# Two transformer layers on one core: a new written-out order for all queues, the alternate homes and the PSUM banks

## The chip, the core and the metric

One NeuronCore of a Trainium2 chip runs the program. It has five engines that each work through a queue of their own in order: PE (TensorE, matmuls), ACT (ScalarE, exponentials and gelu), DVE (VectorE), POOL (GpSimd) and SP (SyncE, which here only issues DMAs). They wait for each other through semaphores. The metric is the device time of one execution in microseconds (us); three runs of the kernel before took 441.66, 441.85 and 443.46 us, median 441.85.

## The reference

One attention block and one MLP block, applied twice with the same weights, each behind a layernorm without scale and with a residual sum. There are 2,048 tokens of width 512, 32 heads of 16, and an MLP of width 1,792. Each token attends to itself and the 255 tokens before it.

```python
def attn(x):                                   # A_x: 1 x 2048 x 512, bfloat16
    q, k, v = heads(x @ wqkv)                  # 32 heads of 16
    s = where(0 <= i - j < 256, q @ k.T / 4, -1e9)
    return merge(softmax(s) @ v) @ wo
def mlp(x):
    return gelu_tanh(x @ w1 + b1) @ w2 + b2    # 512 -> 1792 -> 512

x = A_x
for _ in range(2):
    x = x + attn(layernorm(x))
    x = x + mlp(layernorm(x))
```

## The kernel before, in words

The tokens stand as 16 tiles of 128; two layers make 32 tile steps, numbered tau. Attention goes by blocks of two tiles: 16 blocks b, eight of each layer. The MLP goes by ten jobs J of two or four tiles.

The function writes the program down as 3,098 steps with names (keys), each with what it reads and writes. The keys, with the lines of the profile:

- `bs`, `ba` (L599, L601): statistics of a layernorm on DVE; `vp`, `pw` (L611, L617): its inverse root, the first on POOL or DVE, the second on POOL; `xn` (L627): the normalised tile on DVE.
- `tx` (L632): a DMA that transposes `xn` into xnTA (for attention) or xnTB (for the MLP); for the first and last tiles `tp` (L639) on PE and an evacuation `te` instead.
- `q`, `k`, `v` (L653, in `lnq` and `kv`): projections on PE, followed by `qe`, `ke`, `ve` (L588 or L590, L687), which take them out of PSUM; `vs` (L702): two DMAs that swap the halves of V.
- `scB_G` (L754): scores of block B, visit G. A visit fills four PSUM banks; two exponentials `ex` (L761, ACT) empty them; `mk` (L782, DVE or POOL) multiplies by the mask. A block has ten visits (five at the start of a layer).
- `pv` (L804): the product with V, for half a block; then `od`, `rc`, `nm`, `ot` (L813 to L827): transpose, reciprocal of the row sums, normalisation (DVE or POOL), transpose back; `op` (L653): the output projection; `rs` (L849): the residual sum.
- `mJ_F` (L653): first MLP product of job J for the 128 columns F of 14; `gb` and `ga` (L871, L874): bias on DVE, then gelu on ACT for columns 0 to 5; `ge` (L879): bias and gelu on ACT for the others.
- `y` (L653) and `ya` (L894): second MLP product and residual sum; `xb` (L887, POOL): residual plus bias beforehand; `out` (L898): the store. Of the last tile, tau 31, `y`, `ya` and `out` are cut into two halves of 256 columns, `y31_0` and `y31_256`.
- `ld...`: loads; `ldx` of the input, `ldw` of wqkv, `ldwo`, `ldu0` to `ldu2` the three pieces of W1 (columns F 0 to 5, 6 to 9, 10 to 13), `ldz0` to `ldz3` the four of W2.
- `warm`: 18 matmuls on zeros, of 512 or 32 columns, that read gT and write a PSUM bank nobody uses.

The order of all this isn't found at run time. Three lists are written out: `_ORDER` gives the sequence in which steps are put on their engines' queues, `_ALT` the steps that go to their second home (masks, normalisations and layernorm additions have DVE and POOL, evacuations DVE and ACT), `_BANKS` the PSUM bank of each group in that order. `_Plan.run` reads them:

```python
        for i in _ALT:
            nodes[i]["eng"], nodes[i]["fn"] = nodes[i]["alts"][1]
        banks = iter(_BANKS)
        ...
        for i in _ORDER:
            nd = nodes[i]
            assert nd["deps"] <= seen
            seen.add(i)
            for g, k in nd["alloc"]:
                b = next(banks)
```

`_Sched.op` then gives every step the waits that its reads, writes and bank demand. A step that waits holds up everything behind it on its engine. All 160 DMAs stand in SP's queue.

## Time and profile before

| | |
|---|---|
| median of three runs | 441.85 us |
| span of the profiled execution | 442.4 us |
| PE busy | 416.1 us (94%) |
| ACT busy | 386.4 us (87%) |
| DVE busy | 341.0 us (77%) |
| POOL busy | 212.7 us (48%) |
| DMA | 23.25 MB, 53 GB/s in the mean, 202 GB/s in the first 48 us |

The profiled execution is one of its own, 0.55 us (0.1%) above the median of the three runs. Its page gives busy time by engine, then the chain that ended last, then groups of instructions. In the chain's and groups' lines a tile's name stands for all its buffers; many operations of PE have line 653, since one helper records them all. Idle time of an engine is put down to what ended it. Loads of ACT's function tables are instructions of their own there, 1.28 us each.

### The profile page before, as it was taken

Reading aid. Unit: us, or ns where it says so; the run is one execution under the profiler, and the core shown is the slowest. Engines: PE = TensorE matmul, PEld = TensorE weight load, DVE = VectorE, ACT = ScalarE, POOL = GpSimd, SP = SyncE. Lnnn points to the kernel's source line nnn. Section 1 sums busy time; section 2 is a strip of 40 time slices with the busy share of each in tenths; the row PEclk is TensorE's granted clock in tenths of the full one; section 3 lists DMA queues with packets and bytes.
Section 4 is the critical chain, followed back from the end, with each engine's and each line's share of the span. In section 5 each row is a group of like instructions: output and inputs, shape, how many; then the busy total and the mean of one; then the engine's idle time right before and its main releaser. Section 6 shows DMA issues by size and latency. Waiting matters only on the chain.

```text
span 442.4 us, 16864 instructions
## 1 busy us (share of the span) xinstructions
PE 416.1 (94%) x7523; PEld 233.2 (53%) x7593; DVE 341.0 (77%) x638; ACT 386.4 (87%) x458; POOL 212.7 (48%) x236
## 2 busy tenths in 40 slices
PE   8997999988789997999999999999999999999997
PEld 4555657544444563554455455455555464444675
DVE  7997789788785599967698868877888576746762
ACT  4997999999889999889899989999897988999533
POOL 3566344363442674711575454634728165804411
PEclk9999999999899999999999999999999999999999
DMA  7686422004101012121031021100421014003002
GB/s 234 184 209 185 87 64 45 20 10 69 39 3 25 16 34 56 28 46 24 4 65 31 1 57 26 34 20 10 69 39 20 20 39 105 14 1 81 15 0 73
DMA packets 48116, 23.25 MB, mean 53 GB/s; under 512 B 33196, under 2 KB 48044, under 8 KB 48044
## 3 DMA queue, kind: packets, MB, share of 16 engines
q1 hardware_dynamic: 48044, 22.17, 22.2%
q8 instruction: 60, 0.98, 0.9%
q14 instruction: 12, 0.10, 0.1%
HBM read 8.00 MB, written 2.10 MB: 23 GB/s over the span
## 4 chain that ended last, share of the span: by engine, by line
PE 79%; ACT 11%; DVE 6%; issue 2%; DMA 1%; DVEq 0%
PE ps L653 59%; PE ps L754 9%; PE ps L804 9%; ACT E L761 9%; DVE OD L813 1%; PE ps L539 1%; DVE stat L599 1%; DVE X L849 1%; DMA xnTB<-xn 1%; ACT gT L879 1%; ACT L879 1%; DVE KT L687 1%; DVE E L782 0%; PE ps L639 0%; ACT QT L590 0%
## 5 line engine op out<-in xcount | busy, mean ns | idle before, releaser
L761 ACT ACTIVATE E<-ps 128x1024 bf16<-128x1024 f32 x300 | 284.2, 1033 | 28.7 <-PE ps L754 28.0
L782 POOL TENSOR_TENSOR E<-E,mask 128x512 bf16<-128x512 bf16 (+2 forms) x111 | 120.9, 1106 | 91.3 <-ACT E L761 91.0
L653 PE MATMUL ps<-W_sb,gT 128*128 128x512 bf16 (+1 forms) x434 | 112.2, 373 | 3.2 <-issue 2.2
L653 PE MATMUL ps<-xnTB,W_sb 128*128 128x512 bf16 (+1 forms) x541 | 107.8, 336 | 3.4 <-issue 1.8
L653 PEld LDWEIGHTS ps<-xnTB,W_sb 128*128 128x128 bf16 x560 | 52.0, 98 | 42.9 <-issue 4.1
L653 PE MATMUL ps<-xnTA,Wqkv_sb 128*128 128x256 bf16 x512 | 70.7, 273 | 0.9 <-ACT E L761 0.4
L782 DVE TENSOR_TENSOR E<-E,mask 128x512 bf16<-128x512 bf16 (+2 forms) x125 | 60.1, 500 | 13.3 <-ACT E L761 12.9
L754 PE MATMUL ps<-QT,KT 32*128 32x128 bf16 (+3 forms) x1920 | 60.3, 231 | 9.8 <-ACT E L761 5.6
L653 PEld LDWEIGHTS ps<-W_sb,gT 128*128 128x128 bf16 x462 | 41.2, 98 | 41.1 <-issue 3.6
L754 PEld LDWEIGHTS ps<-QT,KT 32*128 32x128 bf16 x1920 | 28.5, 92 | 59.1 <-ACT E L761 34.9
L653 PEld LDWEIGHTS ps<-xnTA,Wqkv_sb 128*128 128x128 bf16 x512 | 47.4, 98 | 20.2 <-issue 2.9
L813 DVE STREAM_TRANSPOSE OD<-ps 128x1024 f32<-128x1024 f32 x32 | 39.9, 1246 | 21.3 <-PE ps L804 20.7
L887 POOL TENSOR_TENSOR Xb<-X,b2all 128x512 f32<-128x512 bf16 x32 | 37.7, 1180 | 34.3 <-DVE X L894 33.9
L879 ACT ACTIVATE gT<-ps,b1T 128x512 bf16<-128x512 f32 (+1 forms) x80 | 42.6, 609 | 9.5 <-PE ps L653 9.4
L804 PE MATMUL ps<-E,Va 64*17 64x128 bf16 (+3 forms) x1920 | 44.3, 234 | 1.9 <-issue 0.8
L821 POOL TENSOR_TENSOR Nb<-OD,Rc 128x512 bf16<-128x512 f32 x25 | 26.4, 1058 | 38.7 <-DVE Rc L817 29.8
L804 PE MATMUL ps<-E,Vs 64*17 64x128 bf16 (+3 forms) x1920 | 44.9, 234 | 0.0
L599 DVE BATCH_NORM_STATS2 stat<-X 128x6 f32<-128x512 bf16 x64 | 42.9, 679 | 0.5
L804 PEld LDWEIGHTS ps<-E,Va 64*17 64x17 bf16 x1920 | 37.2, 85 | 11.6 <-issue 9.0
L871 DVE TENSOR_SCALAR gT<-ps,b1T 128x512 bf16<-128x512 f32 (+1 forms) x60 | 36.8, 632 | 6.6 <-PE ps L653 6.2
L687 DVE TENSOR_TENSOR KT<-ps,parmask 128x1024 bf16<-128x1024 f32 x32 | 38.7, 1211 | 3.6 <-PE ps L653 3.6
L804 PEld LDWEIGHTS ps<-E,Vs 64*17 64x17 bf16 x1920 | 38.0, 85 | 0.2
(55 smaller groups left out, 348.8 us busy)
## 6 DMA issues: line engine op xcount, KB each, us to landing
Vs<-Va SPq DMA_DIRECT2D x64, 68.0 KB, 2.0
W_sb<-in_B_w_dram SPq DMA_DIRECT2D x4, 512.0 KB, 4.8
out_dram<-X SPq DMA_DIRECT2D x15, 128.0 KB, 1.8
X<-in_A_x_dram SPq DMA_DIRECT2D x3, 512.0 KB
Wqkv_sb<-in_A_wqkv_dram SPq DMA_DIRECT2D x4, 256.0 KB, 4.5
W_sb<-in_B_w_dram SPq DMA_DIRECT2D x2, 384.0 KB, 7.1
W_sb<-in_B_w_dram SPq DMA_DIRECT2D x1, 768.0 KB, 5.0
Wqkv_sb<-in_A_wqkv_dram SPq DMA_DIRECT2D x1, 512.0 KB, 6.7
```

The costliest lines, as they stand in the source:

```text
L599: add("dve", lambda e, B, t=t, k6=k6: e.bn_stats(stat6[:, k6, :], X[:, t, :]), reads=["X%d" % t], writes=["st%d" % k6], key="bs%d" % (k + j))
L653: r = e.matmul(ps[:, B[g][0], cols], lhsT, rhs, start=st, stop=sp)
L687: add("dve", lambda e, B, g=g, i=i: e.tensor_tensor(out=KT[:, kb, 2 * i : 2 * i + 2].rearrange("p c m a q -> p a (c m) q"), in0=ps[:, B[g] ...
L754: x = e.matmul(ps[:, bk[r], o : o + n], KT[rows, kb, c, m].rearrange("p a q -> p (a q)"), QT[rows, c, q : q + n], start=True, stop=True)
L761: add("act", lambda e, B, g_=g_, gi=gi: e.activation(E[:, 2 * gi : 2 * gi + 2, e0 : e0 + 512], ps[:, B[g_][0] : B[g_][0] + 2, :], AF.Exp, ...
L782: fn = lambda e, B: e.tensor_tensor(out=Ew, in0=Ew, in1=Mw, op=ALU.mult)
L804: x = e.matmul(ps[32 * r : 32 * r + VW, B[g][par], c % 2 * 2 * P + lo : c % 2 * 2 * P + hi], V[rows, (2 * b + m // 2) % VR, c * HC + 2 * r ...
L813: add("dve", lambda e, B: e.transpose(OD[:, s].rearrange("p a c q -> p (a c q)"), ps[:, B[g][0] : B[g][0] + 2, :]), reads=["ps:" + g], wri ...
L821: return e.tensor_tensor(out=Nb[:, s, :].rearrange("p (k a d) -> p a k d", a=2, d=Dh), in0=sums[:, :, :, 0:Dh], in1=rc[:, :, :, None].to_b ...
L871: add("dve", lambda e, B, g=g, fc=fc: e.tensor_scalar(out=gT[:, fc, c0 : c0 + M], in0=ps[:, B[g][0], 0:M], scalar1=b1T[:, fc : fc + 1], sc ...
L879: add("act", lambda e, B, g=g, fc=fc: e.activation(gT[:, fc, c0 : c0 + M], ps[:, B[g][0], 0:M], AF.Gelu_apprx_tanh, bias=b1T[:, fc : fc + ...
L887: add("pool", lambda e, B, t=t, xs=xs: e.tensor_tensor(out=Xb[:, xs, :], in0=X[:, t, :], in1=b2all[:], op=ALU.add), reads=["X%d" % t, "b2a ...
```

## The change

All three lists are replaced; the function that writes the steps down, `_Plan` and `_Sched` stay. The diff is numbers alone:

```diff
@@ -165,200 +165,193 @@
 _ORDER = [
-    15, 34, 5, 0, 6, 14, 35, 7, 33, 28, 38, 29, 47, 8, 18, 23, 9, 36, 3, 26, 31, 10, 57, 37, 11, 22, 1, 40, 4, 24,
-    2, 58, 59, 61, 17, 42, 62, 21, 60, 65, 41, 63, 19, 64, 68, 55, 32, 66, 107, 39, 69, 67, 20, 105, 50, 70, 3097,
-    48, 30, 27, 53, 25, 106, 108, 71, 109, 49, 72, 110, 73, 16, 74, 114, 81, 75, 82, 111, 83, 84, 115, 85, 86, 116,
...
+    34, 15, 0, 8, 35, 27, 25, 32, 20, 9, 38, 1, 16, 37, 2, 24, 10, 36, 31, 11, 40, 57, 12, 33, 17, 13, 41, 23, 5, 58,
+    4, 59, 3, 61, 21, 14, 62, 29, 42, 60, 65, 63, 19, 47, 64, 6, 68, 66, 39, 107, 67, 69, 28, 105, 70, 22, 50, 108,
+    30, 81, 106, 82, 109, 7, 83, 110, 84, 71, 72, 3097, 111, 73, 74, 114, 112, 85, 75, 86, 87, 115, 88, 116, 89, 113,
...
 ]
 
 _ALT = [
-    67, 70, 75, 102, 109, 116, 121, 148, 165, 170, 185, 192, 198, 202, 211, 216, 337, 342, 370, 374, 378, 384, 389,
-    393, 398, 402, 406, 407, 412, 421, 437, 554, 571, 576, 585, 590, 595, 608, 609, 613, 634, 654, 687, 691, 696, 710,
...
+    67, 70, 75, 95, 109, 116, 121, 165, 170, 185, 192, 198, 202, 211, 337, 342, 370, 374, 379, 383, 389, 393, 398,
+    406, 412, 437, 534, 567, 571, 580, 581, 590, 595, 599, 603, 608, 609, 618, 634, 654, 691, 696, 719, 724, 911, 916,
...
 ]
 
 _BANKS = [
-    0, 1, 0, 1, 0, 2, 3, 2, 3, 5, 7, 0, 6, 5, 3, 2, 5, 4, 2, 4, 2, 3, 3, 5, 0, 1, 2, 6, 1, 5, 2, 4, 6, 1, 0, 2, 4, 6,
-    0, 2, 7, 5, 4, 6, 2, 0, 2, 4, 6, 4, 0, 7, 2, 3, 0, 4, 6, 0, 4, 2, 3, 4, 6, 0, 1, 4, 5, 2, 6, 0, 6, 7, 4, 2, 0, 2,
...
+    5, 7, 6, 4, 0, 6, 0, 4, 7, 6, 7, 6, 1, 3, 2, 6, 0, 7, 2, 3, 0, 5, 1, 2, 6, 1, 4, 0, 1, 4, 6, 3, 0, 2, 4, 6, 7, 0,
+    2, 4, 5, 6, 2, 0, 2, 4, 7, 4, 0, 6, 2, 0, 0, 4, 3, 6, 2, 0, 4, 3, 4, 6, 0, 1, 5, 4, 2, 6, 0, 4, 2, 7, 2, 0, 4, 6,
...
 ]
```

Read back through the keys it comes to this. The number and kind of steps stay: 1,629 on PE and 160 on SP in both, ACT 439 and then 438, DVE 638 and then 646, POOL 232 and then 225. 122 steps have another home: 88 masks (45 from POOL to DVE, 43 back), 12 normalisations (nine to DVE, three to POOL), 11 layernorm additions, 11 evacuations. 233 of the 658 PSUM groups have another bank. Along PE's queue 1,015 of the 1,629 steps can be kept in their mutual order, along ACT's 351 of the 433 that are on it in both, along DVE's 360 of 581, POOL's 111 of 173, SP's 74 of 160. No PE step moves by more than 140 places.

Some places, before (-) and after (+):

```diff
 PE, around 40 us of the old timeline
-pv1_0 q3_0.3 k3_1.0 k3_1.1 q3_1.0 k3_1.2 q3_1.1 sc1_6 k3_1.3 q3_1.2 q3_1.3 sc1_7 v6.0-3 v7.0-3 sc1_8 m0_2.0
+pv1_0 sc1_6 q3_1.0-3 k3_1.0-3 sc1_7 v6.0-3 v7.0-1 sc1_8 v7.2-3 warm2 m0_4.0
 DVE, around 36 us
-mk1_4_0 rs1 rs0 bs33 bs32 ba33 ba32 ke3_0 xn32 xn33 od1_0
+mk1_3_1 rs1 rs0 bs33 mk1_4_0 bs32 ba33 ba32 ke3_0 xn33 xn32 bs10 od1_0
 SP, from its 20th DMA on
-vs2_1 ldu2 ldwo tx6 vs2_0 ldb2 tx7 vs3_1 vs3_0 ldu0 ldu1 ldz3 vs5_1 tx32 tx33 ldz0 ldz1 vs4_0 tx8 vs6_1 tx9
+vs3_0 vs2_1 ldwo vs3_1 tx6 tx7 vs2_0 ldz0 ldu2 ldu0 tx33 tx32 ldu1 vs4_1 ldz1 vs5_1 vs6_0 ldz2 ldz3 tx9 tx8
 PE, around 114 us
-k7_0.0-3 sc4_5 sc4_6 q7_0.0-3 sc4_7 pv4_0
+k7_0.1 sc4_5 k7_0.2 q7_0.0 k7_0.3 sc4_6 q7_0.1-3 sc4_7 pv4_0
 PE, its end
-y31_256.6-8 y31_0.6-8 y31_256.9 y31_0.9-13 y31_256.10-13 y30.0-13
+y30.5-12 y31_256.6 y31_0.6 y31_256.7 y30.13 y31_0.7 y31_256.8 y31_0.8 y31_256.9-13 y31_0.9-13
 SP, its end
-out11 out5 out15_0 out9 out12 out15_256 out7 out13 out14
+out13 out9 out2 out11 out4 out14 out15_256 out15_0
```

355 rows, old and new, of tables (_ALT, _BANKS, _ORDER) are left out of this document.

## The prediction

> **What bounds the kernel now.** I read the page first: span, busy time by engine, the chain that ended last, the costliest groups.
>
> ```profile
> span 442.4 us, 16864 instructions
> ...
> PE 416.1 (94%) x7523; PEld 233.2 (53%) x7593; DVE 341.0 (77%) x638; ACT 386.4 (87%) x458; POOL 212.7 (48%) x236
> ...
> PE 79%; ACT 11%; DVE 6%; issue 2%; DMA 1%; DVEq 0%
> ...
> L761 ACT ACTIVATE E<-ps 128x1024 bf16<-128x1024 f32 x300 | 284.2, 1033 | 28.7 <-PE ps L754 28.0
> ```
>
> TensorE (PE) is busy 94% of the span and makes up 79% of the chain, so at most 442.4 - 416.1 = 26.3 us can be won without taking matmuls away, and the change takes none away. ScalarE (ACT) comes next; its 300 exponentials alone are 284.2 us. A mean over the span hides where the 26.3 us lie, so the second view is the busy time by stage. Its columns are the stage, its length, then busy time of PE, PE's weight loads, VectorE (DVE), ACT and GpSimd (POOL), the granted clock, the DMA share and GB/s.
>
> ```profile
> 0.00:48.00 48.00, 42.70 (x687) 26.73 (x692) 41.92 (x83) 39.60 (x50) 26.23 (x41) 1.00 0.77 202
> 48.00:84.00 36.00, 34.94 (x704) 23.66 (x708) 29.56 (x59) 34.45 (x49) 13.57 (x14) 1.00 0.21 46
> 84.00:120.00 36.00, 30.30 (x697) 16.72 (x701) 29.21 (x57) 34.14 (x38) 18.08 (x21) 0.95 0.21 36
> 160.00:192.00 32.00, 28.81 (x754) 16.37 (x737) 29.94 (x56) 28.39 (x31) 19.28 (x22) 1.00 0.20 34
> 240.00:340.00 100.00, 97.77 (x1752) 51.38 (x1768) 81.72 (x147) 91.11 (x103) 53.70 (x59) 1.00 0.17 30
> ```
>
> PE idles 5.3 us in the first 48, 5.7 us between 84 and 120, 3.2 us between 160 and 192, but only 2.2 us in the 100 us from 240 on. So there are three stages in which an order can win or lose anything, and a long rest in which PE is already full. Between 84 and 120 ACT has 34.14 of 36 us: ACT sets the pace there. In the first stage DMA moves 202 GB/s and DVE is busy 87%: copies and DVE can hold things up.
>
> **The change, part by part.** No step is added or removed: all 3,098 steps, ACT's 19 table switches, counted in both lists, and the 160 DMAs stay. What moves are the places in the queues, the engine of 122 steps, and PSUM banks. I laid the two lists beside each other, queue by queue.
>
> *Places on PE and ACT.* The coarse order is kept: counted in PE work, the starts and ends of all attention blocks stand within 1.5 us of their old place, and 351 of ACT's 433 common steps keep their order. Of the long PE waits in the stages from 84 to 120 and from 160 to 192, nearly all have the same neighbours in both lists. What matters is thus local.
>
> First, the start. The timeline (start, length, engine, line, operation, and in brackets the idle time before it):
>
> ```profile
> 29.62 1.94 SPq L569 DMA_DIRECT2D W_sb<-in_B_w_dram  x2
> ...
> 37.23 0.74 DVE L627 TENSOR_SCALAR xn<-X,statmv,rstd 128x512 bf16<-128x512 bf16 x2
> 37.71 2.96 SPq L632 DMA_TRANSPOSE xnTB<-xn  x2
> ...
> 40.28 0.40 PE L754 MATMUL ps<-QT,KT 32*128 32x192 bf16 x12 [1.23 <-ACT E L761]
> ...
> 43.58 0.60 PE L653 MATMUL ps<-xnTB,W_sb 128*128 128x256 bf16 x4 [0.73 <-DMA xnTB<-xn]
> ...
> 45.02 3.77 ACT L761 ACTIVATE E<-ps 128x1024 bf16<-128x1024 f32 x4 [0.18 <-PE ps L754]
> ...
> 46.80 2.78 PE L653 MATMUL ps<-xnTB,W_sb 128*128 128x256 bf16 x24
> ```
>
> The 1.23 us wait at 40.28 is the scores visit sc1_7, held by the exponential of sc1_6. The new list puts sc1_6 ahead of eight projection steps and sc1_7 behind them: sixteen matmuls of 256 columns, of which 24 take 2.78 us in the row at 46.80, so some 1.9 us of PE work where three such steps stood. Most of the 1.23 us goes. But next in line stands the first MLP matmul at 43.58, which waits for the transposed copy of the layernorm (xnTB). That copy hangs on DVE and on the DMAs, not on PE: PE would arrive earlier and wait longer. So the saving is between 0 (copy as late as now) and 1.2 us (copy as much earlier). I take 0.3, near the low end, because the new DVE list puts a mask between the two layernorm statistics ahead of the copy, and the new SP list has some 0.77 MB less queued ahead of it (W1's second piece, 512 KB, and two pieces of W2 of 384 KB out, one of 512 KB in); the two roughly cancel.
>
> *Places on SP.* Loads are exchanged with copies. The one that can hurt: the second piece of W1 (512 KB, key ldu1) was issued at the end of the pair at 29.62. Now it stands behind the two transposing copies that wait for DVE. Its landing times, and those of the copies:
>
> ```profile
> W_sb<-in_B_w_dram SPq DMA_DIRECT2D x4, 512.0 KB, 4.8
> ...
> W_sb<-in_B_w_dram SPq DMA_DIRECT2D x2, 384.0 KB, 7.1
> ```
>
> ```profile
> DMA to landing us min/median/max: 2.4/2.5/4.1
> ```
>
> And the largest mask on DVE, the kind that now stands ahead of the copies:
>
> ```profile
> L782 DVE TENSOR_TENSOR E<-E,mask 128x768 bf16<-128x768 bf16 x47 | 26.0, 571 | 8.3 <-ACT E L761 8.2
> ```
>
> The copies' issue ends at 37.71 + 2.96 = 40.7; with the mask ahead (0.57) at 41.2. From there the piece lands between 46.0 (4.8) and 48.3 (7.1). The matmuls that need it run at 46.80, or 47.4 if the copies come 0.57 later. So it costs between nothing and 0.9 us (1.5 if only the piece is late). I take 0: the row of the same size, 4.8, leaves 0.8 us. [...]
>
> Second, the stage that ACT paces:
>
> ```profile
> 85.33 17.81 ACT L761 ACTIVATE E<-ps 128x1024 bf16<-128x1024 f32 x19 [0.53 <-PE ps L754]
> ...
> 107.70 8.46 ACT L761 ACTIVATE E<-ps 128x1024 bf16<-128x1024 f32 x9 [0.22 <-PE ps L754]
> ...
> 121.30 3.77 ACT L761 ACTIVATE E<-ps 128x1024 bf16<-128x1024 f32 x4 [1.78 <-PE ps L754]
> ```
>
> ```profile
> 114.38 0.40 PE L754 MATMUL ps<-QT,KT 32*128 32x256 bf16 x8 [1.25 <-ACT E L761]
> ```
>
> The visit that waits 1.25 us (sc4_6) now has three projection steps between itself and the visit before it, where it had none: six matmuls, 0.7 us by the row at 46.80. That fills PE's wait, but ACT runs without a break from 107.70 to 116.16 around it, and what PE does earlier here it lacks at the next visit. The bounds are 0.75 us won, if ACT got its gaps of 0.22 and 0.53 back, and 0; ACT's unbroken rows are the nearest: 0.
>
> Third, the tail:
>
> ```profile
> 437.26 3.25 SPq L898 DMA_DIRECT2D out_dram<-X  x7
> ```
>
> ```profile
> 439.39 0.69 DVE L894 TENSOR_TENSOR X<-Xb,ps 128x512 bf16<-128x512 f32 x1 [2.20 <-PE ps L653]
> ```
>
> ```profile
> L894 DVE TENSOR_TENSOR X<-Xb,ps 128x256 bf16<-128x256 f32 x2 | 0.8, 418 | 4.2 <-PE ps L653 4.2
> ```
>
> ```profile
> out_dram<-X SPq DMA_DIRECT2D x15, 128.0 KB, 1.8
> ...
> out_dram<-X SPq DMA_DIRECT2D x2, 64.0 KB, 1.7
> ```
>
> Now the last matmuls are those of token tile 30, then one DVE addition of 0.69 us, the last of seven stores, its landing of 1.8. In the new lists tile 30 is interleaved with the two halves of tile 31, and a half comes last: an addition of 0.42 us and a store of 64 KB. That wins 0.69 - 0.42 = 0.27 us in the addition and 1.8 - 1.7 = 0.1 in the landing. The store of the other half is issued just ahead (seven in 3.25 us, 0.46 each), and the last may wait behind it for some 0.1. I take 0.25; the bounds are 0.37 and, if the wait behind the other store is longer, 0.
>
> *Other homes.* 45 masks go from POOL to DVE and 43 the other way, nine normalisations to DVE and three to POOL, eleven evacuations cross with net one off ACT, and eleven tiny layernorm additions cross.
>
> ```profile
> L782 POOL TENSOR_TENSOR E<-E,mask 128x512 bf16<-128x512 bf16 x57 | 66.3, 1172 | 52.7 <-ACT E L761 52.7
> ```
>
> ```profile
> L782 DVE TENSOR_TENSOR E<-E,mask 128x512 bf16<-128x512 bf16 x59 | 29.6, 513 | 4.7 <-ACT E L761 4.6
> ...
> L821 DVE TENSOR_TENSOR Nb<-OD,Rc 128x512 bf16<-128x512 f32 x7 | 5.1, 736 | 0.2
> ```
>
> ```profile
> L821 POOL TENSOR_TENSOR Nb<-OD,Rc 128x512 bf16<-128x512 f32 x25 | 26.4, 1058 | 38.7 <-DVE Rc L817 29.8 <-DVE statmv L601 8.9
> ```
>
> Multiplied out by form, POOL gets 6.5 us less, DVE 5.2 more, ACT 0.7 less. DVE's part by stage of the old timeline: +1.8 up to 48, +1.2 from 84 to 120, +2.4 from 120 to 160, 0 from 160 to 192, -3.6 from 192 to 240, +3.2 from 240 to 340. DVE has idle time in each (6.1, 6.8 and 18.3 us in the first, third and last of the stages shown), and that hides it: 0 on the path. Without that cover it costs up to those sums, and a norm that is 0.3 us shorter on DVE gives some back.
>
> *Banks.* 233 of 658 groups get another bank. Looking up for each group who frees its bank and how much PE work lies between, the number of PE steps with under 0.5 us of work ahead of a release or operand is 11 in both; under 1.5 us 171 before and 188 after. Slightly tighter, not loose: 0.
>
> Sum: -0.3 - 0.25 and zeros, about -0.55 us on the profiled 442.4; the span is 0.55 above the median 441.85 of the runs shown, which I carry over: 441.3.
>
> **The rivals.**
>
> *The clock does not dip (faster).* At 116.5 the granted clock falls to half for 3.4 us. In the view by microsecond the clock is the third column from the right:
>
> ```profile
> 113.00:114.00 1.00, 0.13 (x8) 0.00 (x0) 0.72 (x3) 1.00 (x2) 0.33 (x1) 1.00 0.00 0
> ...
> 117.00:118.00 1.00, 1.00 (x78) 0.91 (x64) 0.00 (x0) 1.00 (x2) 0.00 (x0) 0.50 0.13 30
> 118.00:119.00 1.00, 1.00 (x72) 0.73 (x55) 0.00 (x0) 1.00 (x2) 0.32 (x1) 0.50 0.00 0
> ...
> 126.00:127.00 1.00, 0.41 (x14) 0.17 (x14) 1.00 (x3) 0.85 (x2) 0.00 (x0) 1.00 0.00 0
> ```
>
> Half of 3.4 us is 1.7, and ACT's 1.78 us wait at 121.30 follows directly. The new order puts matmuls into the empty microsecond at 113, and that may keep the clock. Together with the copy 0.9 us earlier (the upper part of its bound) and the tail, 441.85 - 1.7 - 0.9 - 0.25 = 439.0. Against it: PE's work in that window is set by ACT and stays about the same. [...]
>
> [...] Each further dip costs the same 1.7 us; two give 441.3 + 3.4 = 444.7. It decides from the second on. For it: thin stretches as at 113 and 126 remain, and the second one has no dip now; against it: there is one dip in the whole trace.
>
> *DVE takes POOL's place as the late one (slower).* Place: up to 48 and 84 to 120, where DVE heads the chains, with 1.8 + 1.2 = 3.0 us more. If that reaches PE and ACT whole, ACT's unbroken rows carry it on: 441.3 + 3.0 = 444.3. It decides when over 2.7 of it arrives. Speaks for it: DVE then has 43.7 of 48 us; against: part of the added work are masks that PE wants later.
>
> *W1's second piece is late.* Copies 0.57 later and the piece 0.9 behind them: 442.8 with the 0.3 and the tail still won, which is within the bound below.
>
> **How the numbers follow.** A difference under 0.5% (2.2 us) is about what a measurement of this kernel can't tell from none. The forecast, 441.3, has 0.42; W1's piece late (442.8) 0.08; the clock without a dip (439.0) 0.23; DVE late (444.3) 0.18; two more dips (444.7) 0.09. That gives 0.23 faster, 0.50 within, 0.27 slower. The likeliest case's own range is 440.0 to 442.8. For 8 in 10 I go from 438.6 (the faster case with all of the 1.2 us) to 445.2 (the slower cases and half a microsecond).
>
> **What would show it.** The wait before the score matmul near 40 shrinks while the one for xnTB near 43 grows; if both shrink, the 0.3 was too small. W1's second group (m0_8) starts without a wait on W_sb; a wait there is the SP rival. ACT's row from 85 on stays unbroken. DVE's busy total is near 346 and POOL's near 206, with PE's waits on DVE unchanged. The clock column shows where it falls below 1.00. The last store has 64 KB, and the end follows the last matmul by 2.8 us in place of 3.0. The prediction is wrong if the long PE-bound rest (240 to 438), which I count as unchanged, gains or loses more than a microsecond through waits that the old trace does not have.

## The result and the profile after

The new lists make the kernel slower: 445.53 us median of five runs (445.41 to 446.31) against 441.85, a ratio of 1.0074 with a 95% interval of 1.0054 to 1.0093. On another occasion the same kernel took 444.86 us beside 442.55, 1.0053 (1.0037 to 1.0069). The loss is thus half a per cent to three quarters, 2.3 to 3.7 us. The forecast was 441.3; 445.53 lies 0.3 us above its range, and the sign is that of "slower", which had 0.27.

The page of the kernel after, its span, busy times and chain:

```profile
span 443.8 us, 16934 instructions
...
PE 426.3 (96%) x7593; PEld 232.1 (52%) x7593; DVE 346.8 (78%) x646; ACT 386.3 (87%) x457; POOL 205.4 (46%) x229
...
PE 74%; ACT 16%; DVE 5%; DMA 3%; issue 1%; SPq 0%; POOL 0%
```

DVE and POOL moved as worked out (346 and 206 were expected). The chain has more ACT (16% for 11%) and DMA (3% for 1%). PE's busy time can't be laid beside the 416.1 of before: that profile holds 7,523 of the 7,593 matmuls, the others are missing from it. A second profile of the kernel before (run e1_before_again below), with all of them, has PE busy 423.4 us in a span of 440.3, and shows the old kernel better. Its busy times by stage, columns as in the prediction:

```profile
0.00:48.00 48.00, 43.33 (x696) 26.96 (x697) 42.57 (x85) 40.16 (x50) 26.20 (x41) 1.00 0.77 204
48.00:84.00 36.00, 35.77 (x707) 23.32 (x705) 29.52 (x58) 34.44 (x49) 13.57 (x14) 1.00 0.21 44
84.00:120.00 36.00, 31.25 (x717) 16.59 (x715) 30.18 (x58) 34.01 (x39) 18.70 (x22) 1.00 0.19 36
160.00:192.00 32.00, 29.34 (x676) 15.45 (x675) 30.13 (x58) 28.82 (x32) 18.27 (x21) 1.00 0.21 37
240.00:340.00 100.00, 99.98 (x1747) 51.34 (x1745) 81.23 (x144) 91.05 (x103) 53.65 (x58) 1.00 0.18 31
```

The same stages of the kernel after:

```profile
0.00:48.00 48.00, 44.64 (x719) 27.55 (x720) 43.23 (x91) 40.42 (x50) 23.27 (x38) 1.00 0.73 201
48.00:84.00 36.00, 35.65 (x701) 23.04 (x689) 30.55 (x54) 34.12 (x48) 17.13 (x19) 1.00 0.29 44
84.00:120.00 36.00, 30.86 (x714) 16.22 (x707) 31.32 (x61) 33.45 (x38) 12.14 (x15) 1.00 0.23 40
160.00:192.00 32.00, 28.91 (x669) 15.41 (x670) 29.09 (x55) 28.08 (x31) 18.52 (x22) 1.00 0.26 39
240.00:340.00 100.00, 98.89 (x1757) 50.89 (x1746) 82.40 (x151) 88.15 (x99) 49.49 (x52) 1.00 0.16 30
```

The reader is to see three things. PE does 1.3 us more in the first 48 us: the start did get better. Between 240 and 340 the old kernel had 99.98 of 100 us of PE work, so this stage had nothing to win, and the new one lost 1.1 us there. And the old kernel's clock column is 1.00 between 84 and 120, where the profile of the prediction showed 0.95.

Where PE waits, by the operand of the group of matmuls (line, busy and mean ns, then the idle time ahead of them), before:

```profile
L653 PE MATMUL ps<-xnTB,W_sb 128*128 128x512 bf16 (+1 forms) x560 | 111.6, 337 | 1.1 <-DMA xnTB<-xn 0.7 <-ACT E L761 0.4
L754 PE MATMUL ps<-QT,KT 32*128 32x128 bf16 (+3 forms) x1920 | 60.1, 231 | 8.2 <-ACT E L761 4.8 <-DVE Rc L817 1.0 <-DVE gT L871 0.8
...
L804 PE MATMUL ps<-E,Va 64*17 64x128 bf16 (+3 forms) x1920 | 43.2, 230 | 1.7 <-issue 0.8 <-DVE E L782 0.5 <-ACT QT L590 0.2
```

and after:

```profile
L646 PE MATMUL ps<-xnTB,W_sb 128*128 128x512 bf16 (+1 forms) x560 | 113.6, 337 | 2.0 <-DMA xnTB<-xn 1.0 <-issue 0.7 <-DVE E L775 0.2
L747 PE MATMUL ps<-QT,KT 32*128 32x128 bf16 (+3 forms) x1920 | 60.6, 231 | 6.6 <-ACT E L754 2.8 <-DVE Nb L814 1.7 <-DVE Va L581 0.8
...
L797 PE MATMUL ps<-E,Va 64*17 64x128 bf16 (+3 forms) x1920 | 44.0, 230 | 3.1 <-DVE E L775 0.6 <-DVE statmv L594 0.5 <-ACT QT L583 0.5
```

The scores wait 1.6 us less. The first MLP products (xnTB) wait 0.9 more and the products with V (Va) 1.4 more. The view names only gaps between instructions; what a matmul loses while it is stretched isn't in it. So I also took the end of each of PE's 1,629 steps from the trace, subtracted the usual length of such a step, and put the excess down to whichever of its operands came last, by that operand's own end or landing. From 28 us on, in us:

| what came last | before (e1) | after | after again (e13) |
|---|---|---|---|
| a transposing copy | 0.82 | 2.54 | 3.04 |
| nothing: a product with V whose operands were there 0.25 us earlier | 0.40 | 2.06 | 2.04 |
| nothing: step m2_3.3 alone | 0 | 0.49 | 0.59 |
| ACT | 7.83 | 8.90 | 7.65 |
| DVE | 6.48 | 5.19 | 4.39 |
| end of the last matmul | 437.24 | 441.23 | 439.16 |
| from there to the end of the span | 3.06 | 2.57 | 2.54 |

The two profiles of the kernel after agree in the first three rows, and there it waits longer: 4 us in all, of which up to 2 come back on DVE. A longer wait isn't yet a loss, since the time may be covered by another engine. The experiments ask whether these rows are causes, and what makes them. Two groups in them belong to a cause that comes up last, late instruction pages: of ACT's row the waits at the scores step sc4_2 (1.0, 1.8 and 1.3 us in the three columns, in part), and of the second row some 0.5 us at pv1_1 in both profiles of the kernel after.

### The profile page after: what moved, and what is told of

It reads as the page before. It is cut to its first block, busy times and chain, and to the rows that moved or that the text cites. A ratio compares the mean times of both kernels' runs of the same rounds, so it can differ in the third digit from the quotient of the medians.

```text
span 443.8 us, 16934 instructions
## 1 busy us (share of the span) xinstructions
PE 426.3 (96%) x7593; PEld 232.1 (52%) x7593; DVE 346.8 (78%) x646; ACT 386.3 (87%) x457; POOL 205.4 (46%) x229
## 4 chain that ended last, share of the span: by engine, by line
PE 74%; ACT 16%; DVE 5%; DMA 3%; issue 1%; SPq 0%; POOL 0%
PE ps L646 56%; ACT E L754 11%; PE ps L747 8%; PE ps L797 8%; DMA xnTB<-xn 2%; ACT gT L872 2%; DVE E L775 1%; ACT gT L867 1%; PE ps L532 1%; DMA xnTA<-xn 1%; DVE stat L592 1%; DVE X L887 1%; DVE xn L620 1%; ACT L754 1%; ACT L872 1%
## 5 line engine op out<-in xcount | busy, mean ns | idle before, releaser
L775 POOL TENSOR_TENSOR E<-E,mask 128x512 bf16<-128x512 bf16 (+2 forms) x109 | 118.4, 1098 | 111.9 <-ACT E L754 111.6
L646 PE MATMUL ps<-W_sb,gT 128*128 128x512 bf16 (+1 forms) x462 | 118.0, 374 | 0.0
L646 PE MATMUL ps<-xnTB,W_sb 128*128 128x512 bf16 (+1 forms) x560 | 113.6, 337 | 2.0 <-DMA xnTB<-xn 1.0
L646 PE MATMUL ps<-xnTA,Wqkv_sb 128*128 128x256 bf16 x512 | 72.7, 273 | 1.1 <-ACT xnTA L583 0.4
L775 DVE TENSOR_TENSOR E<-E,mask 128x768 bf16<-128x768 bf16 (+2 forms) x127 | 61.4, 503 | 9.9 <-ACT E L754 9.6
L646 PE MATMUL ps<-Wo_sb,OT 128*128 128x512 bf16 x128 | 37.4, 380 | 0.1
```

The lines of the kernel that those rows point to most:

```text
L646: r = e.matmul(ps[:, B[g][0], cols], lhsT, rhs, start=st, stop=sp)
L775: fn = lambda e, B: e.tensor_tensor(out=Ew, in0=Ew, in1=Mw, op=ALU.mult)
```

## Experiments

Steps are named by their keys. Two theories run through the expectations. By the first (L, where a letter is used), the loss is a handful of single waits, each of which can be repaired where it stands. By the second (N), the lists are balanced so closely that the next late step takes the place of one that is repaired. All ratios are to the kernel before on the same chip.

**How firm the two times are.** The kernel before once more as it is (e1), and later the kernel after as it is (e13); no edit.

> The kernel before, unchanged, for its spans and granted clocks. Theory R (the loss lies in the PE-bound rest) reads the profile of before as disturbed by the half clock at 116 to 120: an execution with clock 1.000 then has a span of 440.0 to 440.4, 442.4 less the 1.7 to 1.8 us of the dip less what follows it, and a time of 441.7 to 442.0, 1.7 above the span as in the kernel after (445.53 against 443.8). Rival: the dip belongs to this order of work; then every execution shows a clock of 0.996 and a span of 442.2 to 442.6, and the time stands 0.5 us BELOW its span, unlike after.

> The kernel after, unchanged. If its first set was typical: 445.3 to 445.8, 0.7 to 0.8% above before, spans near 443.8. Rival (the first set was a bad one, as e9 and e11 hint, both 1.5 us below it with edits worth 0.6 us or less): 444.3 to 445.0, 0.45 to 0.65% above before; then about 1 us of the 3.7 is spread of the same program.

e1: 442.19 us (441.39 to 442.99, ten runs), ratio 0.9998 (0.9988 to 1.0007). Nine of the ten runs have a mean clock of 0.999 or 1.000 and spans of 439.7 to 440.8; one has 0.996 and 441.2. In the profiled run the time is 1.76 us above the span (442.06 and 440.3). So the profile that the prediction rests on (span 442.4, clock 0.95 between 84 and 120) belongs to a run of about 444.2 us, not to the median. By these mean clocks a dip like the one at 116.5 came in one of these ten runs, and the median is a run without it. e13: spans 441.7 to 443.6 at a clock of 0.999 to 1.000. The clock has no part in the loss.

**Which part of the change: homes or order.** One list exchanged:

```diff
 e2: kernel after             e3: kernel before
-_ALT = [new]                -_ALT = [old]
+_ALT = [old]                +_ALT = [new]
```

> The order and the banks of after, with the engines (homes) of before. Theory H (the homes of the 122 steps make the loss, by copies and masks that now end late on the other engine): 441.5 to 442.5. Theory P (places in the queues and banks make it): 445 to 446, as after. If the two were solved together and belong together, the mixture is worse than either: 446 to 449.

> The order and the banks of before, with the homes of after; the reverse of the run with old homes. Theory H: 445 to 446. Theory P: 441.5 to 442.5. If order and homes belong together: 446 to 449.

e2 took 454.94 us, 1.0294 (1.026 to 1.0328); e3 463.41, 1.0484 (1.0444 to 1.0523). In the list of PE's waits (us in total, times, longest), e2 has

```profile
PE ps L797 <- POOL E L775: 3.1, 4, 1.9
```

and e3

```profile
PE ps L747 <- DVE gT L864: 3.5, 3, 1.7
PE ps L646 <- DVE gT L864: 2.6, 3, 1.4
PE ps L646 <- DVE KT L680: 2.5, 2, 1.8
```

The order and the homes only make sense together: either without the other costs 13 to 21 us. That is more than the idle time of an engine lets one expect. DVE has 2 to 19 us idle per stage, and still it is late by up to 1.8 us: the last row of e3 is the evacuation of the K projection (`ke`), which DVE reaches too late in its queue. "DVE has idle time, so the added work is hidden" is no valid step; it says nothing of when. So the change can't be split into a share of the homes and a share of the order.

**Which stretch.** The lists were joined at a cut; every step keeps the home and bank of the list that it comes from.

```diff
 e4
-_ORDER = [new]
+_ORDER = [new, its first 1,600 steps, to 228 us] + [the rest in the old order]
 e6
-_ORDER = [old]
+_ORDER = [old, its first 1,545 steps, to 221 us] + [the rest in the new order]
```

> Up to step 1600 of the list (228 us, all attention blocks up to 9 begun) the order, homes and banks of after, from there those of before. Theory R (the 3.7 us are lost behind 228, where PE is full; the start's 1.5 us are won and given back between 84 and 120): 441.8 to 442.8. Rival S (the stages before 228 lose it, the old profile's dip hiding that): 444.5 to 445.5.

> Order, homes and banks of before up to step 1545 of the list (221 us), where both lists have done exactly the same steps; from there those of after. Against the undisturbed run of before, after's PE is 1.1 us late at that point, 4.0 us late at its end, and ends the tail 0.5 us sooner. Theory W/R (the losses are local and add up): the part behind 221 loses 2.9 - 0.5 = 2.4 us, 444.3 to 445.0. Rival J (parts were fitted to each other, and the joint costs): 446 or more; the run that joined at 228 the other way round lost 1.6 us in the 5 us behind its joint. Rival S (the part before 221 is what loses): 442.0 to 442.8.

e4: 444.16, 1.0044 (1.0027 to 1.0061). Its profiled run is 0.1 us behind e1 at 221 us and 1.7 behind from the joint on; the difference arises at the joint itself, where sc9_6 waits for the residual sum rs17 on DVE, which ends at 231.4 us (229.0 in e1). e6: 443.85, 1.0027 (1.001 to 1.0045). Its front is the old one, and the rest loses: PE's last matmul is 2.1 us later, the tail gains 0.5 back. The excess lies at pv11_1 (0.67 us), m8_6 (0.48), q15_0 (0.35) and four products with V (0.25 each). So the stretch from 221 us on is shown to lose by itself: 1.2 us by the times (0.4 to 2.0), 1.5 by the two profiled spans.

The traces also show where PE stands against e1, at points where both lists have done the same steps of PE (us; minus is ahead):

| e1 is at | after | e13 | e6 |
|---|---|---|---|
| 99.6 | -0.51 | -0.54 | -0.12 |
| 121.1 | +0.02 | -0.51 | -0.10 |
| 190.0 | +1.49 | +0.42 | -0.10 |
| 220.6 | +1.09 | +0.01 | -0.09 |
| 311.5 | +2.51 | +0.75 | +0.85 |
| 437.2 | +3.99 | +1.92 | +2.06 |

Behind 221 us the new order loses 2.9 us in after, 1.9 in e13 and 2.1 in e6. Its front is level in e13 and 1.1 us behind in after, though it is the same kernel: what the front loses differs from run to run.

**The start and the tail alone.** The prediction expected gains there. e8 and e16 take the new list to its 547th step (71 us), then the old one, with two rearranged tails; e12 is the old kernel with the second tail.

```diff
 e12 (SP and PE, end)
-... y31_0.9-13 y31_256.10-13 y30.0-13  ya30  out14
+... y30.0-13  ya30 out14  y31_256.10-13 ya31_256 out15_256  y31_0.9-13 ya31_0 out15_0
```

> Up to step 547 (71 us) order, homes and banks of after, where its PE is 0.4 us ahead of the undisturbed run of before; from there before's, with its last matmuls rearranged so that the two half tiles end (token tile 30's 14 matmuls, its addition and store go ahead of eight matmuls of tile 31), for a last addition of 0.42 instead of 0.69 us and a last store of 64 KB. Theory W/R (gains and losses are local and add up): 0.4 + 0.5 us better than before, 441.1 to 441.6 against 442.2. Rival J (the joint costs what it wins): 442.0 to 443.8.

> Before, with the last 25 matmul steps in another order: token tile 30 ends 11 half-size matmuls ahead of the end, then one half of tile 31, then the other, so that the three additions and stores do not meet. Theory: the span ends 2.55 to 2.65 us after the last matmul, as in after (2.57), in place of 3.06 us, and the time falls by 0.3 to 0.5 us against before. Rival: the last addition and store queue behind the other two as in the run that had them close together (3.1 us): no gain.

> After's list to 71 us, before's from there, and the last 25 matmuls as in the run with the new tail. Each part alone came out at before's time within the interval. Theory: 0.4 us from the start and 0.3 from the tail, 441.5 against 442.2. Rival (what the start wins is lost again at 107 to 120 us, where the first such kernel waited 1.2 us for nothing at v13.1): 442.0 to 442.8.

e8: 442.40, 1.0003 (0.9989 to 1.0017). e12: 442.02, 0.9998 (0.9983 to 1.0013). e16: 442.15, 0.9998 (0.9982 to 1.0014). None differs from before. e12's end follows the last matmul by 2.77 us in place of 3.06, as small as that. The profiled runs of e8 and e16 (443.22 and 444.9 us) are slower than their medians, so they show little of where a lead goes: e8's is gone by 73 us, and e16 is 1.3 us behind at 42. At 106 us both have a further wait. The timeline of e8:

```profile
106.60 0.38 PE L646 MATMUL ps<-Wqkv_sb,xnTA 128*128 128x512 bf16 x1 [1.08 <-issue]
```

This is v13.1, a projection whose operands had been there for long. In e16 it waits some 1.5 us and the clock falls to half for some 3 us (the run's mean clock is 0.996). What such a wait "for nothing" is comes up below.

**Filling the waits.** In e5 steps of the second MLP product are pulled ahead of five waiting steps; e15 does four of the five and also moves a copy (as in e11 below).

```diff
 e5 (PE)                                    e15 (PE): the first four
+y15.10-11        ahead of pv10_0
+y17.8-10         ahead of pv11_1
+y21.5-7          ahead of pv13_0
+y23.13 y22.7-8   ahead of pv14_0
+y25.9-11         ahead of m8_6.0
```

> After, with 14 matmul steps of the second MLP layer, whose operands have long been there, pulled directly ahead of five steps that wait in its trace and did not wait before: pv10_0 (0.26 us), pv11_1 (0.66), pv13_0 (0.27), pv14_0 (0.28) and m8_6 (0.56), together 2.03 us. Theory W (the rest loses by steps of PE that stand too close behind their operands): the five waits go and stay gone, span 443.8 - 2.0 = 441.8, time 443.3 to 443.8. Rival N (what is late next takes their place: PE only arrives earlier at the next late operand): 444.8 to 445.6. Rival M (the matmul time itself grew): no change, 445.5.

> After, with the copy tx61 ahead of the store and eleven matmul steps of the second MLP layer ahead of pv10_0, pv11_1, pv13_0 and pv14_0 together. Theory W: 0.56 + 0.66 (when the mask of POOL wins) + 0.2 to 0.8, less what is late next (0.5 in the run with five waits filled): 1.0 to 1.5 us below after, +0.2 to +0.45% of before. Rival N (all of it is taken by the next late operand): as after.

e5: 444.79, 1.0051 (1.0035 to 1.0067). The five waits went, and sc13_7 (0.53 us), sc14_8 (0.37), m7_5 (0.30) and sc10_7 (0.22) came. e15: 445.84, 1.0071 (1.0055 to 1.0088), not faster than after. In it the copies' row of the table is down to 1.7 us from 2.5, and ACT's is up to 10.4 from 8.9. Filling a wait where ACT sets the pace a few steps later only moves it: the second theory is what e5 and e15 show, and the first is refuted as a way to win the time back by filling waits. Both times lie between the two of after, 1.0053 and 1.0074.

**The longer products with V.** They wait for many semaphores. In e9 the waits for the V copies are already made in earlier steps, by reads added to them:

```diff
+        steps = {nd["key"]: nd for nd in PL.nodes}
+        for step, names in (("y0.9", ["VT4"]), ("y0.10", ["VT5"]), ("k11_0.2", ["VS9"]), ...):
+            steps[step]["reads"] += names
```

> After, with the semaphore waits of seven products of probabilities and values (pv) on the shifted value copies, landed 0.5 to 26 us earlier, put one by one on matmul steps 1 to 14 steps ahead of them; nothing else moves. In after's trace pv2_0, pv9_0, pv10_0, pv12_0, pv13_0 and pv14_0 each take 0.19 to 0.33 us longer than the 1.37 us of the kind although every operand had arrived 0.28 to 1.0 us before. Theory A (5 to 7 waits at one step cost their own time once PE has little work queued): these extras, 1.6 us in all, go, time 444.0 to 444.5. Rival I (PE stands for its instructions inside the step; the rows show the breaks at its 72nd to 127th pair, behind the waits): extras and time unchanged, 445.3 to 445.8.

444.05, 1.0053 (1.0028 to 1.0079). pv10_0's excess went; pv9_0 (0.30 us), pv12_0 (0.27), pv13_0 (0.25), pv14_0 (0.28) stay. The number of waits isn't their cause. In these steps the gap lies in the middle, between the 72nd and the 127th pair of weight load and matmul, where no wait stands. The shifts below leave it in place too. So the cause of this row is open, but for the 0.5 us at pv1_1: some 1.1 us.

**A mask on DVE beside POOL.** pv11_1 waits 0.66 us for mk11_7_1, a mask that the change moves from POOL to DVE. The timeline of after (start, length, engine, line, operation):

```profile
306.13 2.31 POOL L775 TENSOR_TENSOR E<-E,mask 128x512 bf16<-128x512 bf16 x2
306.14 1.28 DVE L775 TENSOR_TENSOR E<-E,mask 128x256 bf16<-128x256 bf16 x1
...
307.52 0.28 PE L797 MATMUL ps<-E,Va 64*17 64x256 bf16 x4 [0.61 <-DVE E L775]
```

The mask takes 1.28 us, and in e7, where two POOL masks are put later, 0.28:

```diff
 e7 (POOL)
-mk12_0_0 mk12_1_0 ... mk12_2_1
+... mk12_2_1 mk12_0_0 mk12_1_0
```

> After, with two masks of POOL (mk12_0_0, mk12_1_0, at 306.1 to 308.5, not needed before 317) put behind POOL's next one, so that POOL is idle from 306.2 to 309. Theory L (a mask on DVE cannot run while POOL has one: mk11_7_1, moved to DVE, took 1.28 us beside them and ended 0.14 us after the first of them; other masks of its form take 0.28): it takes 0.3 to 0.45, pv11_1's wait of 0.66 shrinks to 0.2 or less, and the time falls by up to 0.5 us, 445.0 to 445.3. Rival Q (its length has another cause, or the wait comes from DVE's queue ahead of it): 1.28 us again, wait and time unchanged, 445.5.

```profile
304.50 0.28 DVE L775 TENSOR_TENSOR E<-E,mask 128x256 bf16<-128x256 bf16 x1
...
307.33 2.93 POOL L775 TENSOR_TENSOR E<-E,mask 128x256 bf16<-128x256 bf16 x3 [2.82 <-ACT E L754]
307.88 2.54 DVE L620 TENSOR_SCALAR xn<-X,statmv,rstd 128x512 bf16<-128x512 bf16 x2
```

pv11_1's wait fell from 0.66 to 0.02 us, as expected of the cause. But the kernel got slower, 446.69, 1.0096 (1.0077 to 1.0115): the last row shows two normalised tiles (`xn`) of 0.41 us each taking 2.54 beside the POOL masks in their new place, and downstream q13_1 waits 1.9 us and m6_0 2.5. In after, POOL's first mask ends at 307.28 and DVE's at 307.42, 0.14 later: DVE's operation waited for POOL's to end, it wasn't slowed in part. The trace has 19 operations of DVE that are over 0.15 us longer than the others of their form. Each ends 0.15 us (masks of 256 columns, `xn`), 0.28 (masks of 512), 0.42 (a mask of 768) or 0.55 (`nm`) behind the end of the POOL operation beside it, however long it takes. So masks of 256 columns go from 0.28 us to as much as 1.29, `xn` from 0.41 to as much as 0.88, and `nm` from 0.68 to 1.28. `bs` and `ot` are not longer (0.68 and 0.70 us with and without POOL), nor are those that read PSUM (`ke` 1.22 us, `od` 1.25, with and without). The old kernel has about 19 such collisions, worth some 9 us of DVE's time, the new one 19 worth some 10.5; only this one became a wait of PE, and not in every run. In e13, the same kernel, the two masks start at 305.03 (DVE) and 305.02 (POOL), and DVE's takes 0.28 us.

**A copy behind a store.** m8_6.0 waits 0.56 us for its transposed copy. The timeline of after, SP's queue and PE:

```profile
407.76 0.33 SPq L891 DMA_DIRECT2D out_dram<-X  x1
408.14 1.19 SPq L625 DMA_TRANSPOSE xnTB<-xn  x1
...
411.99 0.60 PE L646 MATMUL ps<-xnTB,W_sb 128*128 128x256 bf16 x4 [0.40 <-issue]
```

Its source was ready at 405.06. SP had the store out10 ahead of the copy, and out10 waits for ya26, which ended at 407.70. e11 exchanges the two:

```diff
 e11 (SP)
-out10 tx61
+tx61 out10
```

> After, with the last but one transposing copy (tx61) moved ahead of one output store (out10) on SP's queue. In after's trace its operand was there at 405.06 but the store ahead waited until 407.70 for an addition, the copy landed at 411.89 and m8_6 waited 0.56 us; in before it landed with 5 us to spare. Theory W: the wait of m8_6 goes, 0.4 to 0.6 us less, 445.0. Rival N: the next late operand takes it: 445.5.

```profile
404.25 1.19 SPq L625 DMA_TRANSPOSE xnTB<-xn  x1
406.84 0.33 SPq L891 DMA_DIRECT2D out_dram<-X  x1
```

The wait went: 444.07, 1.004 (1.002 to 1.0061), against 1.0053 and 1.0074 for after. The intervals overlap, so the half microsecond is shown by the trace and only suggested by the times; the other late copies took some 0.8 us more in this run. Those are tx43 (m3_2, 0.98 us in after), tx51 (m5_1, 0.38), tx54 (m6_0, 0.36, behind the 2.05 us that SP takes to issue tx55) and tx16 (k8_0, 0.26). They were not moved one by one, and only tx61 is shown behind a store. tx16 and tx43 lie in the front (155 and 174 us). Two of the others belong to the new list's front, not to their own place: in e6, with the old front, m5_1 and m6_0 do not wait, m8_6 does.

**Waits for nothing: instruction pages.** m2_3.3 waits half a microsecond between two steps of the same kind, with all operands there. The timeline of after:

```profile
119.15 0.40 PE L747 MATMUL ps<-QT,KT 32*128 32x192 bf16 x12
119.88 0.61 PE L646 MATMUL ps<-xnTB,W_sb 128*128 128x512 bf16 x2 [0.33 <-issue]
...
120.68 0.41 PE L747 MATMUL ps<-QT,KT 32*128 32x128 bf16 x24 [0.20 <-ACT E L754]
```

A DMA queue of its own moves instructions; its row on the profile's page:

```profile
q8 instruction: 60, 0.98, 1.0%
```

60 transfers, 0.98 MB, so 16 KB each; PE's list has 15,351 instructions (7,593 matmuls, as many weight loads and 165 instructions that wait), 256 for each transfer. In after and the runs with shifted lists below, PE's single waits of 0.4 us and more with all operands there stand, nearly all, at instruction 190 to 193 of a block of 256, and end 1.2 to 1.7 us after a transfer of this queue landed. Laid over PE's instruction times, each transfer starts 0.4 us or more after PE is at instruction 160 of a block, mostly 0.5 to 2.6, and takes 0.9 to 1.8 us. From these times I estimate that a page is asked for at about instruction 160 and first used 286 instructions later, where the waits stand; the trace doesn't show the asking itself. A half block's product with V is some 258 instructions in 1.37 us. Where one lies in between, 286 instructions could pass in 2.8 to 3.7 us, and the waits stand behind such stretches.

By its place the kernel after has a second such wait, at sc4_2: instruction 192 of its block, where m2_3.3 has 191. The list of waits puts it down to the last engine that it can name, DVE (that is all of the 1.7 <-DVE Nb in the row of the scores above), but sc4_2's last operand was there 1.1 us before. The timeline of after, PE and ACT:

```profile
106.51 0.40 PE L747 MATMUL ps<-QT,KT 32*128 32x192 bf16 x12 [1.70 <-DVE Nb L814]
...
106.96 8.36 ACT L754 ACTIVATE E<-ps 128x1024 bf16<-128x1024 f32 x9 [0.70 <-PE ps L747]
```

Here ACT, which sets the pace in this stage, stands still for it, 0.70 us in after. In e13 PE waits 0.7 us and ACT 0.25:

```profile
106.48 8.36 ACT L754 ACTIVATE E<-ps 128x1024 bf16<-128x1024 f32 x9 [0.25 <-PE ps L747]
```

If late pages are the cause, moving PE's list by a few instructions must move these waits. Four kernels do nothing else:

```diff
 e10: after, ahead of PE's first step (40 waits that are satisfied early)
+        def idle_waits(e):
+            for n in range(40):
+                e.wait_ge(S_.cnt_sem["pool" if n % 2 else "dve"], 1)
 e14: after, e18: before: one of the 18 warm-up matmuls becomes eleven of 32 columns (+20 instructions)
-            add("pe", lambda e, B, ...: e.matmul(ps[...], gT[...], gT[...]), key="warm%d" % h)
+            def warm(e, B, times=11 if h == 14 else 1):
+                for k in range(times):
+                    x = e.matmul(ps[...], gT[...], gT[...])
 e17: after, four of the warm-up matmuls of 32 columns left out (-8 instructions)
-        return _ORDER
+        return [i for i in _ORDER if nodes[i]["key"] not in ("warm9", "warm14", "warm16", "warm17")]
```

> After, with 40 waits on events long past at PE's very start, where it idles for 1.5 us: some 20 instructions more, so that every later instruction stands 20 further in PE's pages of 16 KB (256 instructions). Theory I (PE stands still where a page comes late, because a dense step of 256 instructions lies between its request and its use): the wait of 0.5 us for nothing at m2_3.3 (119.8 us; 191 instructions into a page, as was v13.1 in the run that waited 1.1 us there) goes or moves, and some extras of the pv steps change by over 0.1 us; time within 0.7 us of after either way. Rival A (they are waits for operands or for the waits themselves): the same steps wait the same time within 0.05 us.

> After, with eleven small warm-up matmuls in place of one at 6.8 us, where PE then idles 0.41 us for the first projection (ten pairs, 20 instructions, 0.3 us): the schedule stays, each later instruction stands 20 further in its page of 256. Theory I (waits without an operand are late instructions): the waits at m2_3.3 (0.48 to 0.59 us in five traces of this list) and in the middle of pv1_1 (0.4) go or move elsewhere; new ones of 0.3 us and more may stand at steps without waits, as m3_4.1 (1.0) and y1.2 (1.4) in e10; the time may move by 1 us to either side. Rival: these waits stay within 0.1 us, time as after.

> The kernel after without four of its eighteen warm-up matmuls (of 32 columns, on zeros), so that PE's list is eight instructions shorter ahead of the first real matmul. Computed from the instruction times of the kernel after: the shortest stretch between the point that asks for an instruction page and the point that uses it is 2.88 us now (the one that ends at m2_3.3) and would be 4.45 us, so no matmul waits for a page. Theory of the pages: m2_3.3's wait of 0.49 us goes and no new wait without an operand over 0.3 us comes; at most 0.5 us of time is won, 444.4 to 445.2, ratio 1.004 to 1.006, because the rest of the loss (copies, masks, longer products with V) stays. Rival, any shift of PE's list costs 4 to 6 us as the one of 20 did: 449 or more.

> The kernel before with the same twenty more instructions on PE at the start (eleven small warm-up matmuls in place of one) that cost the kernel after 4 to 6 us. Theory of the pages: what a shift costs hangs on where the list's dense stretches fall. Computed from the old kernel's instruction times, its shortest stretch would go from 3.20 to 2.78 us, ahead of sc1_6 near 38 us, with seven more under 3.5 us; so waits without an operand of 0.3 us to 1.5 us come, at sc1_6, near 51 (m0_13), near 105 (sc4_1) or near 119 us (sc4_8), and the time is 443 to 448. If the loss of the kernel after under the shift were a matter of its list alone, the kernel before would stay at 442.2 with a margin of 0.5 us.

e10: 452.76, 1.0235 (1.0208 to 1.0261); it starts 2.1 us later, m2_3.3's wait falls to 0.10, and y1.2 (1.36 us), sc4_1 (2.26) and m3_4.1 (1.00) wait with operands there. e14: 450.97, 1.019 (1.0162 to 1.0219); y1.2 1.45 and sc4_1 2.14 us, then m3_2 1.37. e18: 451.30, 1.0191 (1.0168 to 1.0215): the kernel before is hit as hard, 9 us by twenty small instructions in the first 9 us. In e18 the largest waits fall at sc1_6 (1.98 us), sc4_1 (1.6), m0_13.0 (1.26) and behind m3_0.3 (1.10), with smaller ones at sc4_8 (0.6), m3_9 (0.5) and sc10_0 (0.37), all of them at the place in a block that is given above. (In this kernel the added lines move line 653 to 658 and 754 to 759.) Its timeline at sc1_6 and at sc4_1:

```profile
37.99 0.39 PE L759 MATMUL ps<-QT,KT 32*128 32x256 bf16 x5
40.09 0.28 PE L759 MATMUL ps<-QT,KT 32*128 32x256 bf16 x3 [1.72 <-issue]
...
109.80 0.39 PE L759 MATMUL ps<-QT,KT 32*128 32x256 bf16 x7 [1.55 <-issue]
```

In the first, one step of eight matmuls stands still after its fifth. And the view by microsecond, further on:

```profile
111.00:112.00 1.00, 0.59 (x14) 0.37 (x15) 0.45 (x1) 1.00 (x2) 0.00 (x0) 0.99 0.71 143
112.00:113.00 1.00, 1.00 (x4) 0.40 (x3) 0.39 (x1) 1.00 (x3) 0.74 (x1) 0.50 0.38 81
113.00:114.00 1.00, 1.00 (x4) 0.15 (x1) 0.31 (x1) 1.00 (x2) 1.00 (x2) 0.50 0.14 29
```

The clock (third column from the right) goes to half, here and after sc1_6. In e14, at half clock, a projection of 512 columns takes 0.61 us (at 109.20), where the one of e8 at 106.60 takes 0.38. PE is behind e1 by 2.4 us at 42 us, 5.9 at 112, 8.0 at 218, and 8.9 at the end: the loss grows where these waits are and hardly afterwards.

e17 asked for the other direction: by the times of after none was to be left under 4.45 us. This leaves out sc4_2, whose stretch is as short as m2_3.3's (2.8 us). e17: 444.45, 1.0054 (1.004 to 1.0067), and the timeline:

```profile
106.57 0.38 PE L747 MATMUL ps<-QT,KT 32*128 32x192 bf16 x9 [0.46 <-issue]
...
119.21 0.31 PE L747 MATMUL ps<-QT,KT 32*128 32x192 bf16 x8
119.45 0.61 PE L646 MATMUL ps<-xnTB,W_sb 128*128 128x512 bf16 x2
120.65 0.41 PE L747 MATMUL ps<-QT,KT 32*128 32x128 bf16 x24 [0.59 <-DVE gT L864]
```

m2_3.3 follows at once. The scores behind it start at 120.65, where after had 120.68: the exponential ahead of them ends when it did. So the page wait at m2_3.3 is real and costs nothing, because ACT's end covers it. The wait at sc4_2 didn't go: it moved into the step, behind its third matmul (first row), and ACT still stands 0.36 us for it; pv2_0 is stretched by 0.59 us, and pv1_1 still waits 0.3 at the same place in its block. e17 is thus not a kernel without late pages, and no run of the new list is. Late pages explain what shifts cost, and they stand where parts of two lists were joined (v13.1 in e8 and e16). What share of the kernel after's loss they have stays open; sc4_2's is part of the difference between after and e13 in the table of PE's standing above. The rows of late copies and of the longer products with V behind 221 us are no such waits.

## Why the prediction was wrong

**The step that failed** is the one it named itself: the rest from 240 to 438 us counted as unchanged, on the ground that the coarse order is kept and that the added DVE work is hidden. e6 shows this rest (with 20 us more) to lose 1.2 us by its times on its own, 1.5 by its profile, and in after and e13 PE falls 2.9 and 1.9 us behind there, through waits that the old trace does not have: a copy that SP issues behind a waiting store (m8_6), a mask on DVE that comes late (pv11_1), longer products with V. The prediction counted on SP only the loads that move past copies in the start. The copies tx16, tx43, tx51, tx54 and tx61, later in the queue, were moved as well and got no term; they are worth 1.7 to 2.2 us by the table, of which tx16 and tx43 belong to the front, which was not counted to lose either. How much of these waits is loss was shown for none but tx61, and there only by the trace; the cause of the longer products with V stays open. For the one followed to its cause, SP's queue would have shown it: out10 with its wait for ya26 stands ahead of tx61 in the new list alone.

**"2.2 us idle between 240 and 340".** This was read as a small reserve. It was missing records: with all matmuls there the stage has 99.98 of 100. A stage without idle time can only lose by a change of order, and a count of instructions beside the busy time (x7523 and x7593) warns of this.

**Start, -0.3.** The direction was right, the size too small by the prediction's own test: both waits shrank. sc1_7's went from 0.66 us (e1; 0.28 of it with its operand there, a late page) to 0.25, that for the copy xnTB from 0.82 to 0, and sc2_0 ended 0.9 us earlier (46.22 and 45.33). But it is no gain at the end. PE is half a microsecond ahead at 99.6 us in after and e13. In after this goes at sc4_2, by the late page; in e13 it is still there at 121 us, and goes by 190, with m3_2's late copy tx43. So the lead survived the stage that ACT paces in one of the two runs, and was lost to waits that the prediction did not count. e8 and e16, which keep this start, measure no gain.

**W1's second piece, 0.** Right: it landed at 44.18 us, and m0_8.0 ended at 45.64 without a wait for it.

**The ACT stage, 0.** Right for the visit it was worked out for. sc4_6's wait fell from 1.35 us to 0.31, the next one, sc4_7, grew from 0.52 to 0.74, and the visit ended 0.2 us earlier. This is what "what PE does earlier here it lacks at the next visit" said. The sign that ACT's row stays unbroken from 85 us on did not come: it has gaps in e1 too, and in after a new one of 0.70 us ahead of sc4_2's exponential. ACT is busy 33.45 us between 84 and 120 in place of 34.01.

**Tail, -0.25.** Right in kind; it measured -0.49. The timelines' last DVE and SP rows, before (e1):

```profile
435.14 3.25 SPq L898 DMA_DIRECT2D out_dram<-X  x7
437.26 0.69 DVE L894 TENSOR_TENSOR X<-Xb,ps 128x512 bf16<-128x512 f32 x1 [2.20 <-PE ps L653]
```

and after, where three additions stand in one row:

```profile
434.15 7.94 SPq L891 DMA_DIRECT2D out_dram<-X  x8
439.91 1.77 DVE L887 TENSOR_TENSOR X<-Xb,ps 128x512 bf16<-128x512 f32 x3 [5.79 <-PE ps L646]
```

**Homes, 0.** The totals came out (DVE +6.0 against e1, +5.2 expected), the cover did not hold everywhere: mk11_7_1 with 0.66 us is a home's price in after, by the collision with POOL's mask. e3 shows that the same homes are far from free in the old order.

**Banks, 0.** No run takes the banks alone, so this stays open.

**The carry-over.** "The span is 0.55 above the median" joined two different runs: a time is 1.76 us above its own span, so the profiled run was some 2.3 us above the median. It held a clock dip that the median does not have. The forecast was lucky here, since it stood on the median.

**The rivals.** *The clock does not dip* had nothing to win, for the same reason: nine of e1's ten runs have none. That matmuls in the empty microsecond at 113 keep the clock was an estimate, and what brings a dip is not shown. The two more dips of the slower rival did not come in after (a mean clock of 1.0 in all five runs). The profiled runs of e7, e8, e10 and e16 have 0.996, those of e14 and e18 0.992; in e14 the clock is at half from 109.0 to 112.4 us, after a gap in PE's work of 2.01 us, and in e18 from 112.0 to 115.4, after one of 1.55. After's own gap of 1.70 us at 106.5 had no such fall behind it. *DVE takes POOL's place as the late one* gave 444.3, the right size, in the wrong place and by the wrong engine: DVE's row of the table fell, and between 0 and 48 us PE got faster. The rival that was missing is "SP's queue: a copy that comes late in the new list", with its price per copy, 0.3 to 1 us; a store ahead of it is the reason in one case, tx61. Late instruction pages, whose waits moved in every run with a shifted list (e10, e14, e17, e18), were not a rival either.

## What to carry to other kernels

Where PE is full (99.98 of 100 us here), a new order has nothing to win: go through each DMA in the new queue that a matmul needs, and look at what the DMA ahead of it waits for. A saving in an early stage counts only if no later wait takes it, and idle time of an engine doesn't make work put on it free: when it is done decides (e2 and e3, 13 to 21 us). A wait is not the fault of the engine that a list of waits names, when that engine was done long before: compare the operand's end with the start, as at sc4_2. Before an order is judged by half a per cent, move the instruction list by a few instructions: if that costs 2%, as here, pages and not the order may be what is measured; one shift that removes one such wait does not settle it.

## What the runs showed of the hardware

- A DMA queue moved 60 transfers of 16 KB for PE's 15,351 instructions, 256 each. In dense stretches (286 instructions in 2.8 to 3.7 us) PE had single waits of 0.3 to 2.3 us with all operands there, nearly all at instruction 190 to 193 of a block and 1.2 to 1.7 us after a transfer landed. Twenty more instructions at the start cost 1.9% in both kernels (e14 and e18).
- A DVE mask that met a POOL mask in after ended 0.14 us behind it: 0.28 us became 1.28. In e11 DVE's mask started at 305.88 and POOL's at 305.87, and DVE's took its 0.28 us; in after 306.14 and 306.13, and it took 1.28. Which of two starts within 10 ns goes first isn't to be read from the trace's start times.
- The clock fell to half for 3.4 us in before at 116.5, after a gap in PE's work of 1.25 us that ended at 114.38, and in e14 at 109.0, after one of 2.01 that ended at 108.80. After has a gap of 1.70 us at 106.5 and no fall.
